# Gated linear attention and an expert layer on one core: TensorE's issue order written out as a pipeline over items, and eight PSUM banks for the later experts

## The chip, the cores and the metric

The kernel runs on one core of a Trainium2 chip. The metric is the device time of one execution in microseconds, the median over several executions. TensorE does the matrix products (its records are PE, its weight loads PEld), VectorE is DVE, ScalarE is ACT, GpSimd is POOL, and SyncE (SP) issues all DMAs of this kernel. Every engine works through its own instruction stream strictly in order, and waits on semaphores where an operand of another engine isn't there yet.

## What is computed

Two steps follow each other, here cut to what matters:

```python
# gated linear attention: q, k, v, f_logit are (4, 8, 768, 48), float32
f = sigmoid(f_logit); state = 0
for t in range(768):
    state = f[t][:, None] * state + outer(k[t], v[t])
    y[t] = q[t] @ state
x = y as (3072, 384)
# experts: w_gate (384, 8), w1 (8, 384, 1024), w2 (8, 1024, 384)
logits = x @ w_gate; P = exp(logits - logits.max())
for _ in range(8):
    P /= P.sum(1); P /= P.sum(0); P *= 3072 / 8
out = sum(P[:, e] * (relu(x @ w1[e]) @ w2[e]) for e in range(8))
```

The normalisation of P couples all tokens: no P is known before the last logits are, so an expert's output can be scaled only after all of the attention.

## The kernel before

**Attention.** The sequence work is cut into 32 items (batch, half of the sequence, pair of heads); four items, 4u to 4u+3, make the unit u of 384 tokens, and there are eight units. Every product of float32 operands is made of three float16 products (high times high, low times high, high times low), which is why most tiles come in pairs, as qh and ql. An item is prepared by `pre` and consumed by `attn`:

- `pre(i)`: ACT takes the sigmoids (L378, L380); DVE scans the decay (`r`, L382), guards and inverts it (`pi`, L384, L385), scales k (L394) and scans a second time (`q`, L386); POOL multiplies `tds` (L387) and q (L388); ACT rounds q to `qh` (L391) and DVE takes `ql` (L392); ACT and POOL make the two parts of k in `kb` (L398, L399), which a transposing DMA turns into `kt` (L401); ACT and DVE make `vh` and `vl` (L403, L404).
- `attn(i)`: 18 score matmuls into `aps` (L416), masked by DVE into `am` (L418) and split into `ah` (ACT, L421) and `al` (POOL, L422); 18 state matmuls into `kvps` (L429), folded by DVE into `ut` (L440), scaled by POOL (L444) and split into `sh` and `sl` (L445, L446); 33 or 36 output matmuls into `yps` (L457), which ACT and DVE evict as `xh` and `xl` (L463, L465).

After its fourth item a unit gets its gate logits (`logits`, L473 to L480): six matmuls over `xh` and `xl`, an ACT copy `lt`, three transposes, a DVE reduction into `lg`. When all eight units are done, `sinkhorn` normalises: eight rounds, each with one matmul (L92) between short DVE operations.

**Experts.** `moe(e, u)` takes expert e over the 384 tokens of unit u: 72 matmuls of 384 columns into eight `hps` tiles (L310), each evicted by ACT into `hh` (L315) and then by DVE into `hl` (L316); then 72 matmuls into three `yps` tiles (L329). I call this a pair, of 144 matmuls; there are 64 pairs. The pairs in RAW (experts 0 and 1, all units) are done before P is known: their result goes unscaled to DRAM (`yr`, `ys`) and is fetched again later (`yb`) and scaled and added. All other pairs add straight from PSUM (L294). The weights are loaded per expert in eight pieces (`load_w1`, `load_w2`) through two raw buffers and split: for experts 0 and 1 by ACT twice and POOL (L262 to L264), later by ACT and DVE (L266, L267), and DVE takes the largest magnitude of each piece (`wmx`, L268).

**What sets the order.** The program is written one step after another, and a scheduler orders each engine's stream by priority. Attention comes first in the text; `W1PRIO`, `W2PRIO` and `E0_HOLD` say how early the weights of experts 0 and 1 come. So the scheduler alone decides where expert matmuls stand between attention matmuls.

**PSUM.** Of eight banks the experts have three (pool `psm`, tag m); attention has five (pool `psa`: one for `aps`, two for `kvps`, two for `yps` and logits), and keeps them to the end of the program.

Of the kernel before, what the change touches and what calls it, by code (L numbers as in the profile page):

```python
# [74 lines left out]
def sinkhorn(nc, pool, psp, tag, identf, onesf, lg, pe):  # L75
# [2 lines left out]
    row = partition_reduce(nc, pool, psp, tag, identf, sm[:, 0:1], ALU.max, "sk")
# [1 line left out]
    nc.tensor.matmul(out=ps, lhsT=onesf[0:1, :], rhs=row, start=True, stop=True)  # L80
# [4 lines left out]
    for it in range(8):  # L85
# [6 lines left out]
        nc.tensor.matmul(out=ps, lhsT=onesf, rhs=cs, start=True, stop=True)  # L92
# [114 lines left out]
def fast(ctx, tc, qkf, vbd, wg, w1, w2, out, flag):  # L207
# [49 lines left out]
    def split_w(raw, e, j, k):  # L257
# [10 lines left out]
        nc.vector.tensor_reduce(out=wmx[:, k - 1, 4 * e + j:4 * e + j + 1], in_=wh.rearrange("p a f -> p (a f)"), axis=AX.X, op=ALU.max, apply_absolute_value=True)  # L268
# [26 lines left out]

    def moe(e, u, w, mode):
# [3 lines left out]
        for f in range(FT):  # L300
            if f % 2 == 0 and len(w1s) <= f // 2:
                with at(W1PRIO[e] if e < 2 else WPRIO + 10 * e):
# [3 lines left out]
            ps = psm.tile([128, HS], F32, name=f"hps_{e}_{u}_{f}", tag="m")  # L306
            n = 0
            for a, x in ((wh, xh), (wl, xh), (wh, xl)):
                for k in range(KT):
                    nc.tensor.matmul(out=ps, lhsT=a[:, k, fs], rhs=x[:, k, :], start=(n == 0), stop=(n == 8))  # L310
# [7 lines left out]
            hl.append(tl)  # L318
        for t in range(TT):
            ts = slice(t * 128, t * 128 + 128)  # L320
            ps = psm.tile([128, DM], F32, name=f"yps_{e}_{u}_{t}", tag="m")
            n = 0
            for f in range(FT):
                if f % 2 == 0 and len(w2s) <= f // 2:
                    with at(W2PRIO[e] if e < 2 else WPRIO + 10 * e):
                        w2s.append(load_w2(e, f // 2))
                wh, wl = w2s[f // 2]
                for a, b in ((hh[f], wh), (hl[f], wh), (hh[f], wl)):
                    nc.tensor.matmul(out=ps, lhsT=a[:, ts], rhs=b[:, f % 2, :], start=(n == 0), stop=(n == 3 * FT - 1))  # L329
# [36 lines left out]
    carry = [ap.tile([R, 96], F32, name=f"carry{p}", bufs=1) for p in range(NP)]  # L366
    tds = cst.tile([R, 32, NC], F32, name="tds")

    def pre(i):
# [12 lines left out]
        nc.vector.tensor_tensor_scan(out=r[:, ::-1], data0=ft[:, :0:-1], data1=ind[:, :0:-1], initial=0.0, op0=ALU.mult, op1=ALU.add)  # L382
# [9 lines left out]
        nc.vector.tensor_tensor(out=ql, in0=fl, in1=qh, op=ALU.subtract)  # L392
# [222 lines left out]
```

## Time and profile before

| | us |
|---|---|
| median of 3 runs (1740.84 to 1743.7) | 1742.46 |
| the profiled execution, its own time | 1744.41 |
| its span, first to last instruction | 1742.7 |
| last attention matmul (a logits transpose, L479) starts at | 385.2 |
| PE, DVE, ACT, POOL busy | 1625.3, 806.5, 476.7, 244.3 |

The span has two parts with different limits: up to about 385 us, where attention and expert matmuls share TensorE and DVE is the busiest engine, and the rest, where expert matmuls stand close together. A matmul's record lasts about 0.33 us, but the next one starts after half of that, since they are pipelined; so the distance from start to start is what counts, not the busy time.

### The profile page before, as it was taken

How to read it: one execution, taken by the hardware profiler on the slowest of the kernel's cores; microseconds unless marked ns; L12 is line 12 of the kernel's file. 1: busy time of each engine (PE TensorE's matmuls, PEld its weight loads, DVE VectorE, ACT ScalarE, POOL GpSimd, SP SyncE). 2: the span in 40 equal slices, each digit the busy share in tenths (PEclk: the TensorE clock that was granted, in tenths of full speed). 3: DMA queues.
4: the chain of work that ended last, by engine and by line, in shares of the span. 5: the costliest groups of instructions: out<-in, count | busy, mean ns of one | idle time of the engine just before them, and what ended most of it. 6: DMA issues, size and time to landing. Idle time of an engine off the chain costs nothing.

```text
span 1742.7 us, 27315 instructions
## 1 busy us (share of the span) xinstructions
PE 1625.3 (93%) x11566; PEld 1002.1 (58%) x11566; DVE 806.5 (46%) x1482; ACT 476.7 (27%) x956; POOL 244.3 (14%) x235
## 2 busy tenths in 40 slices
...
DVE  9999888855523642244222522253224422222222
...
PEclk9989999999999999999999999999999999999999
...
GB/s 178 136 172 142 120 129 109 110 54 29 127 50 73 156 84 1 1 28 46 1 1 1 73 1 1 1 55 19 1 1 28 28 1 1 1 5 24 28 28 29
DMA packets 90452, 90.26 MB, mean 52 GB/s; under 512 B 58960, under 2 KB 74448, under 8 KB 90320
## 3 DMA queue, kind: packets, MB, share of 16 engines
...
q14 instruction: 40, 0.33, 0.1%
...
## 4 chain that ended last, share of the span: by engine, by line
PE 76%; DVE 12%; DMA 5%; issue 2%; ACT 2%; POOL 2%; SPq 0%; ACTq 0%; DVEq 0%; POOLq 0%
PE yps L329 38%; PE hps L310 37%; DMA q<-in_qkf_dram 2%; DVE ql L392 1%; DVE q L386 1%; DMA w2r<-in_w_dram 1%; DVE r L382 1%; DVE vl L404 1%; DVE ut L440 1%; DVE wmx L268 1%; POOL kb L399 1%; DVE hl L316 1%; DVE xl L465 1%; DMA yb<-ys 1%; DVE w2l L267 1%
## 5 line engine op out<-in xcount | busy, mean ns | idle before, releaser
L315 ACT ACTIVATE hh<-hps 128x384 f16<-128x384 f32 x512 | 248.2, 488 | 939.1 <-PE hps L310 937.9
L329 PE MATMUL yps<-w2h,hh 128*128 128x384 f16 x1536 | 501.2, 328 | 0.6 <-DVE hl L316 0.6
L329 PE MATMUL yps<-w2h,hl 128*128 128x384 f16 x1536 | 494.2, 327 | 0.4 <-DVE hl L316 0.4
L329 PE MATMUL yps<-w2l,hh 128*128 128x384 f16 x1536 | 494.2, 328 | 0.0
L316 DVE SCALAR_TENSOR_TENSOR hl<-hps,hh 128x384 f16<-128x384 f32 x512 | 280.9, 555 | 401.4 <-ACT hh L315 400.7
L310 PEld LDWEIGHTS <-w1h 128*128 128x128 f16 x3072 | 301.1, 98 | 224.4 <-issue 32.9
L329 PEld LDWEIGHTS <-hh 128*128 128x128 f16 x3072 | 301.1, 98 | 198.0 <-issue 2.9
L310 PE MATMUL hps<-xh,w1h 128*128 128x384 f16 x1536 | 337.7, 329 | 21.5 <-DVE hl L316 21.2
L310 PE MATMUL hps<-xh,w1l 128*128 128x384 f16 x1536 | 336.9, 328 | 0.0
L310 PE MATMUL hps<-xl,w1h 128*128 128x384 f16 x1536 | 336.5, 328 | 0.0
L294 DVE SCALAR_TENSOR_TENSOR acc<-yps,pes,acc 128x384 f32<-128x384 f32 x144 | 88.9, 617 | 420.0 <-PE yps L329 420.0
L310 PEld LDWEIGHTS <-w1l 128*128 128x128 f16 x1536 | 151.0, 98 | 100.5 <-issue 2.7
L329 PEld LDWEIGHTS <-hl 128*128 128x128 f16 x1536 | 150.9, 98 | 100.5 <-issue 2.3
L399 POOL TENSOR_TENSOR kb<-q,kb 48x384 f16<-48x384 f32 x64 | 75.8, 1185 | 23.5 <-ACT kb L398 21.1
L429 PE MATMUL kvps<-vh,kt 128*128 128x96 f16 x384 | 39.0, 223 | 20.8 <-DVE ut L440 13.4
L429 PEld LDWEIGHTS <-kt 128*128 128x128 f16 x576 | 34.2, 107 | 33.3 <-issue 19.2
L334 ACT ACTIVATE yr<-yps 128x384 f32<-128x384 f32 x48 | 23.4, 486 | 91.5 <-PE yps L329 87.4
L416 PE MATMUL aps<-qh,kb 112*128 112x64 f16 x384 | 27.2, 204 | 21.9 <-ACT qh L391 16.9
L388 POOL TENSOR_TENSOR q<-q 112x384 f32<-112x384 f32 x32 | 44.7, 1396 | 18.9 <-DVE q L386 17.5
L416 PEld LDWEIGHTS <-kb 112*128 112x128 f16 x576 | 25.1, 105 | 38.3 <-issue 35.8
L457 PE MATMUL yps<-al,vh 128*128 128x64 f16 x192 | 35.0, 198 | 12.5 <-POOL al L422 11.9
L440 DVE SCALAR_TENSOR_TENSOR ut<-ut,tds,kvps 112x96 f32<-112x96 f32 x144 | 43.1, 301 | 2.3 <-PE kvps L429 1.3
...
## 6 DMA issues: line engine op xcount, KB each, us to landing
...
w1r<-in_w_dram SPq DMA_DIRECT2D x32, 384.0 KB, 3.3
w2r<-in_w_dram SPq DMA_DIRECT2D x32, 384.0 KB, 3.1
...
vs<-in_vbd_dram SPq DMA_DIRECT2D x4, 384.0 KB, 3.5
```

Source lines behind the costliest of these rows:

```text
L294: nc.vector.scalar_tensor_tensor(out=a, in0=y, scalar=p, in1=a, op0=ALU.mult, op1=ALU.add)
L310: nc.tensor.matmul(out=ps, lhsT=a[:, k, fs], rhs=x[:, k, :], start=(n == 0), stop=(n == 8))
L315: nc.scalar.activation(out=th, in_=ps, func=AF.Relu)
L316: nc.vector.scalar_tensor_tensor(out=tl, in0=ps, scalar=0.0, in1=th, op0=ALU.max, op1=ALU.subtract)
L329: nc.tensor.matmul(out=ps, lhsT=a[:, ts], rhs=b[:, f % 2, :], start=(n == 0), stop=(n == 3 * FT - 1))
L334: nc.scalar.activation(out=yr, in_=ps, func=AF.Copy)
L388: nc.gpsimd.tensor_tensor(out=fl, in0=fl, in1=q, op=ALU.mult)
L399: nc.gpsimd.tensor_tensor(out=kb[rs, 1, :, cs], in0=km[rs], in1=kb[rs, 0, :, cs], op=ALU.subtract)
L416: nc.tensor.matmul(out=aps[:, c, :], lhsT=a[:, c, :], rhs=x[:, cs[c]], start=(n == 0), stop=(n == 2))
L429: nc.tensor.matmul(out=kv[:, c, :], lhsT=ktb[i % 2][:, (a * NC + 3 * g + c) * R:(a * NC + 3 * g + c) * R + 128], rhs=x[:, 3 * g + c, :], s ...
L440: nc.vector.scalar_tensor_tensor(out=un, in0=ut[:, c, :], scalar=td[:, c:c + 1], in1=kv[0:R], op0=ALU.mult, op1=ALU.add)
L457: nc.tensor.matmul(out=yps[:, cs[c]], lhsT=a, rhs=x, start=(n == 0), stop=(n == len(mm) - 1))
```

## The change

1. Every matmul and transpose of the fast path goes through a helper `mm`, which ties it behind the one before it in the text. TensorE's stream is now the order of the text.
2. The text is a loop over items i = 0 to 32. A turn issues the score and state matmuls of item i (`scores`), from turn 5 on 28 expert matmuls, the output matmuls of item i-1 (`outputs`), after every fourth item the logits of the unit, and 28 more expert matmuls. `pre(i+1)` is written between. `moe` became a generator that yields after each matmul; `fill(n)` takes n of them from the RAW pairs.
3. In `sinkhorn`, 22 expert matmuls go ahead of each of its ten TensorE instructions.
4. RAW holds 13 pairs instead of 16 (expert 0 with all units, expert 1 with 0, 1, 2, 4 and 5). The other three pairs of expert 1 come after `sinkhorn` and add straight from PSUM.
5. DVE's first scan of `pre(i)` is tied behind a DVE operation of item i-1: `ql` for i = 1 to 3, `sl` of item 3 for i = 4, `am` of item i-1 from i = 5 on.
6. The 16 `wmx` reductions of experts 0 and 1 move from the place of the weights' loading to behind `pes`, the end of `sinkhorn`. All 16 weight pieces of experts 0 and 1 are issued in turns 0 to 8, with no `hold` and no priority of their own.
7. `psa` is closed when attention ends; five more banks (pool `psb`) go to the experts, which then use eight in turn (`bank`).

```diff
-RAW = [(e, u) for u in range(U) for e in range(2)]
+RAW = [(e, u) for u in range(U) for e in range(2) if e == 0 or u in (0, 1, 2, 4, 5)]
+FILL = 56
+SK_FILL = 22
...
+    def mm(transpose=False, **kw):
+        ins = (nc.tensor.transpose if transpose else nc.tensor.matmul)(**kw)
+        if order:
+            behind(ins, order[-1])
+        order.append(ins)
...
+    def largest(wh, e, j, k):
+        ins = nc.vector.tensor_reduce(out=wmx[:, k - 1, 4 * e + j:4 * e + j + 1], in_=wh.rearrange("p a f -> p (a f)"), axis=AX.X, op=ALU.max, apply_absolute_value=True)
+        if e < 2:
+            behind(ins, held[0])
...
+    def bank(shape, name):
+        n = banks[0]
+        banks[0] += 1
+        if late and n % 8 >= 3:
+            return late[1].tile(shape, F32, name=name, tag="m")
+        return psm.tile(shape, F32, name=name, tag="m")
...
+        if i:
+            behind(scan, done[i - 1])
...
+    for i in range(4 * U + 1):
+        if i < 4 * U:
+            scs[i] = scores(i, sts[i])
+        if i < 4:
+            ws[0][0].append(load_w1(0, i))
+        if i + 1 < 4 * U:
+            sts[i + 1] = pre(i + 1)
+        if 2 <= i < 6:
+            ws[0][1].append(load_w2(0, i - 2))
+        if 5 <= i < 9:
+            ws[1][0].append(load_w1(1, i - 5))
+            ws[1][1].append(load_w2(1, i - 5))
+        if i > 4:
+            fill(FILL // 2)
+        if i > 0:
+            outputs(i - 1, sts.pop(i - 1), scs.pop(i - 1))
+            if i % 4 == 0:
+                logits(i // 4 - 1)
+        if i > 4:
+            fill(FILL - FILL // 2)
+    sinkhorn(nc, cst, psa, "y", identf, onesf, lg, pe, lambda **kw: (fill(SK_FILL), mm(**kw)))
+    held.append(nc.vector.tensor_scalar(out=pes, in0=pe, scalar1=OSC, scalar2=None, op0=ALU.mult))
+    fill(10 ** 6)
     actx.close()
```

Three places in the engines' streams show what moves. Names end in a running number; `_1_0_5` in `hps_1_0_5` is expert 1, unit 0, row group 5. In the changed program every matmul stands under L224, the line of `mm`.

**TensorE, the logits of unit 1.** Before, from the last of the six logits matmuls (`lps1`, over `xl1`) to the transposes of its copy `lt1`:

```order
L473 MATMUL lps1_1120<-xl1_639,wgs_97 128x384
L310 LDWEIGHTS w1l_1_1_4482
L310 MATMUL hps_1_0_2_4487<-xh0_154,w1l_1_1_4482 128x384
L310 LDWEIGHTS w1l_1_1_4482
L310 MATMUL hps_1_0_2_4487<-xh0_154,w1l_1_1_4482 128x384
L310 LDWEIGHTS w1h_1_1_4481
L310 MATMUL hps_1_0_2_4487<-xl0_155,w1h_1_1_4481 128x384
L310 LDWEIGHTS w1h_1_1_4481
L310 MATMUL hps_1_0_2_4487<-xl0_155,w1h_1_1_4481 128x384
L310 LDWEIGHTS w1h_1_1_4481
L310 MATMUL hps_1_0_2_4487<-xl0_155,w1h_1_1_4481 128x384
L479 MATMUL lps21_1129<-identf_83,lt1_1127 128x16 x3
```

Five expert matmuls and their weight loads stood between the two, and others between the logits matmuls themselves. Now, from the last two logits matmuls on:

```order
L224 MATMUL lps1_1611<-xl1_938,wgs_94 128x384
L224 LDWEIGHTS wgs_94
L224 MATMUL lps1_1611<-xl1_938,wgs_94 128x384
L224 MATMUL lps21_1620<-identf_80,lt1_1618 128x16 x3
L224 LDWEIGHTS w1h_1_2_1306
L224 MATMUL hps_1_0_5_1560<-xl0_354,w1h_1_2_1306 128x384
L224 LDWEIGHTS w1h_1_2_1306
L224 MATMUL hps_1_0_5_1560<-xl0_354,w1h_1_2_1306 128x384
L224 LDWEIGHTS w1h_1_3_1513
```

The six logits matmuls follow the output matmuls of the unit's last item directly, and the transposes follow them with nothing between.

**DVE, around item 11.** Before, `ql12` and `ql13` (items 12 and 13) were done ahead of `am_11`, and the first scan of item 14 too:

```order
L392 TENSOR_TENSOR ql_12_1634<-q3_12_1620,qh_12_1633 112x384
L465 SCALAR_TENSOR_TENSOR xl2_1135<-yps_8_1216,xh2_1134 96x384
L418 SCALAR_TENSOR_TENSOR am_10_1412<-aps_10_1393,mask_90 128x384
L446 SCALAR_TENSOR_TENSOR sl0_140<-ut_10_1438,sh0_136 112x480
L404 SCALAR_TENSOR_TENSOR vl0_130<-vr_12_1622,vh0_124 128x576
L392 TENSOR_TENSOR ql_13_1753<-q3_13_1739,qh_13_1752 112x384
L465 SCALAR_TENSOR_TENSOR xl2_1135<-yps_9_1332,xh2_1134 96x384
L442 COPY ut_11_1554<-kvps_11_0_1534 112x96
L316 SCALAR_TENSOR_TENSOR hl_1_0_7_4584<-hps_1_0_7_4573,hh_1_0_7_4583 128x384
L440 SCALAR_TENSOR_TENSOR ut_11_1554<-ut_11_1554,tds_152,kvps_11_0_1534 112x96
L382 SCALAR_TENSOR_TENSOR r_14_1864<-ft0_113,ind_94 112x384
L418 SCALAR_TENSOR_TENSOR am_11_1528<-aps_11_1509,mask_90 128x384
```

Now, in the same place, between the second scan of item 11 and `am_11`:

```order
L474 SCALAR_TENSOR_TENSOR ut_10_1895<-ut_10_1895,tds_152,kvps_10_1_1885 112x96 x2
L474 SCALAR_TENSOR_TENSOR carry2_150<-ut_10_1895,tds_152,kvps_10_1_1885 112x96
L339 SCALAR_TENSOR_TENSOR hl_0_1_0_1952<-hps_0_1_0_1941,hh_0_1_0_1951 128x384
L339 SCALAR_TENSOR_TENSOR hl_0_1_1_1966<-hps_0_1_1_1955,hh_0_1_1_1965 128x384
L423 TENSOR_TENSOR ql_11_1919<-q3_11_1905,qh_11_1918 112x384
L480 SCALAR_TENSOR_TENSOR sl0_140<-ut_10_1895,sh0_136 112x480
L437 SCALAR_TENSOR_TENSOR vl0_130<-vr_12_2108,vh0_124 128x576
L510 SCALAR_TENSOR_TENSOR xl2_1781<-yps_9_1972,xh2_1780 96x384
L339 SCALAR_TENSOR_TENSOR hl_0_1_2_2016<-hps_0_1_2_1969,hh_0_1_2_2015 128x384
L339 SCALAR_TENSOR_TENSOR hl_0_1_3_2030<-hps_0_1_3_2019,hh_0_1_3_2029 128x384
L339 SCALAR_TENSOR_TENSOR hl_0_1_4_2044<-hps_0_1_4_2033,hh_0_1_4_2043 128x384
L450 SCALAR_TENSOR_TENSOR am_11_2070<-aps_11_2051,mask_87 128x384
```

`ql_11` is now the last preparation ahead of `am_11`; the first scan of item 12 comes behind it. Behind `ql_11` stand `sl0`, `vl0`, `xl2` and three evictions `hl` of expert rows.

**DVE, the end of `sinkhorn`.** Before, from `pes` on:

```order
L548 TENSOR_SCALAR pes_104<-pe_103 128x192
L507 TENSOR_REDUCE g_9359<-pe_103 128x1
L292 TENSOR_SCALAR acc0_7447<-yb_0_0_7448,pes_104 128x384 x3
L508 TENSOR_SCALAR ok_9357<-g_9359 128x1
L294 SCALAR_TENSOR_TENSOR acc0_7447<-yb_1_0_7453,pes_104,acc0_7447 128x384 x3
L292 TENSOR_SCALAR acc1_7704<-yb_0_1_7705,pes_104 128x384 x3
L294 SCALAR_TENSOR_TENSOR acc1_7704<-yb_1_1_7710,pes_104,acc1_7704 128x384 x3
L292 TENSOR_SCALAR acc2_7905<-yb_0_2_7906,pes_104 128x384 x3
L294 SCALAR_TENSOR_TENSOR acc2_7905<-yb_1_2_7911,pes_104,acc2_7905 128x384 x3
L292 TENSOR_SCALAR acc3_8106<-yb_0_3_8107,pes_104 128x384
L316 SCALAR_TENSOR_TENSOR hl_0_5_0_6282<-hps_0_5_0_6271,hh_0_5_0_6281 128x384
```

Now `pes` is followed by thirteen `wmx` reductions, of which these are the last ten, and then by the eviction of the last rows of the pair of expert 0 and unit 7:

```order
L285 TENSOR_REDUCE wmx_102<-w1h_0_3_578 128x1
L285 TENSOR_REDUCE wmx_102<-w1h_1_0_881 128x1
L285 TENSOR_REDUCE wmx_102<-w1h_1_1_1103 128x1
L285 TENSOR_REDUCE wmx_102<-w1h_1_2_1306 128x1
L285 TENSOR_REDUCE wmx_102<-w1h_1_3_1513 128x1
L285 TENSOR_REDUCE wmx_102<-w2h_0_0_480 128x1
L285 TENSOR_REDUCE wmx_102<-w2h_0_1_610 128x1
L285 TENSOR_REDUCE wmx_102<-w2h_0_2_733 128x1
L285 TENSOR_REDUCE wmx_102<-w2h_0_3_874 128x1
L285 TENSOR_REDUCE wmx_102<-w2h_1_0_888 128x1
L339 SCALAR_TENSOR_TENSOR hl_0_7_7_6748<-hps_0_7_7_6737,hh_0_7_7_6747 128x384
L285 TENSOR_REDUCE wmx_102<-w2h_1_1_1110 128x1
```

The scaled additions of the fetched results stood here before and now come later; the reductions, which had been spread over the loading of the weights, stand ahead of `hl_0_7_7`.

More of the change, by code (lines that the diff above doesn't have):

```diff
@@ L72, in partition_reduce, with sinkhorn @@
     return row
[L75 removed]
+def sinkhorn(nc, pool, psp, tag, identf, onesf, lg, pe, mm):
     sm = pool.tile([128, 2], F32, name="sk_sm")
     nc.vector.tensor_reduce(out=sm[:, 0:1], in_=lg.rearrange("p a e -> p (a e)"), axis=AX.X, op=ALU.max)
[L78 removed]
+    row = partition_reduce(nc, pool, psp, tag, identf, sm[:, 0:1], ALU.max, "sk", mm)
     ps = psp.tile([128, 1], F32, name="sk_m", tag=tag)
[L80 removed]
+    mm(out=ps, lhsT=onesf[0:1, :], rhs=row, start=True, stop=True)
     nc.vector.tensor_scalar(out=sm[:, 1:2], in0=ps, scalar1=-1.0, scalar2=None, op0=ALU.mult)
@@ L91, in sinkhorn @@
         ps = psp.tile([128, NE], F32, name=f"sk_c{it}", tag=tag)
-        nc.tensor.matmul(out=ps, lhsT=onesf, rhs=cs, start=True, stop=True)
+        mm(out=ps, lhsT=onesf, rhs=cs, start=True, stop=True)
         nc.vector.tensor_scalar(out=cs, in0=ps, scalar1=1e-9, scalar2=None, op0=ALU.add)
@@ L214, in at, with behind @@
         tc.cur_priority = kept
+    order, held = [], []
+    def behind(ins, first):
+        tc.add_manual_dep(
+            ins.ins, first.ins.name,
+            mybir.DependencyInfo(mybir.DependencyClass.NoSync, mybir.DependencyReason.DATA),
+            reason="issue order")
+    def mm(transpose=False, **kw):
[3 more added lines that the diff above has]
+        order.append(ins)
     cst = ctx.enter_context(tc.tile_pool(name="cst", bufs=1))
@@ L381, in pre @@
         r = ap.tile([R, HS], F32, name=f"r_{i}", tag="r")
-        nc.vector.tensor_tensor_scan(out=r[:, ::-1], data0=ft[:, :0:-1], data1=ind[:, :0:-1], initial=0.0, op0=ALU.mult, op1=ALU.add)
+        scan = nc.vector.tensor_tensor_scan(out=r[:, ::-1], data0=ft[:, :0:-1], data1=ind[:, :0:-1], initial=0.0, op0=ALU.mult, op1=ALU.add)
+        if i:
+            behind(scan, done[i - 1])
         r3 = r.rearrange("r (c t) -> r c t", t=C)
@@ L445, in attn, with outputs @@
         nc.scalar.activation(out=sh[:, c0:], in_=ut[:, c0:], func=AF.Copy, scale=SS)
-        nc.vector.scalar_tensor_tensor(out=sl[:, c0:], in0=ut[:, c0:], scalar=SS, in1=sh[:, c0:], op0=ALU.mult, op1=ALU.subtract)
+        ins = nc.vector.scalar_tensor_tensor(out=sl[:, c0:], in0=ut[:, c0:], scalar=SS, in1=sh[:, c0:], op0=ALU.mult, op1=ALU.subtract)
+        if i == 3:
+            done[i] = ins
+        return ah, al, shw, slw, c0
+    def outputs(i, st, sc):
+        u, p = i // 4, i % 4
+        qh, ql = st[2], st[3]
+        ah, al, shw, slw, c0 = sc
+        cs = [slice(c * C, (c + 1) * C) for c in range(NC)]
+        if p == 0:
+            xt[u] = xalloc(u)
         xh, xl = xt[u]
@@ L472, in logits @@
             for k in range(KT):
-                nc.tensor.matmul(out=ps, lhsT=wgs[:, k, :], rhs=x[:, k, :], start=(n == 0), stop=(n == 2 * KT - 1))
+                mm(out=ps, lhsT=wgs[:, k, :], rhs=x[:, k, :], start=(n == 0), stop=(n == 2 * KT - 1))
                 n += 1
```

97 lines of the change are left out of this document (52 added, 45 removed).

## The prediction

> **What bounds the kernel now.** I read the profile's head first, then busy time by stage, then expert matmuls alone before and after the last attention matmul.
>
> ```profile
> span 1742.7 us, 27315 instructions
> DVE  9999888855523642244222522253224422222222
> PEclk9989999999999999999999999999999999999999
> 50.00:100.00 50.00, 30.14 (x324) 21.80 (x323) 47.34 (x81) 27.62 (x53) 36.92 (x37) 0.93 0.55 140
> 385.30:1742.70 1357.40, 1337.74 (x8214) 803.78 (x8212) 472.89 (x848) 273.64 (x532) 0.00 (x0) 1.00 0.10 30
> 0.00:385.30 385.30, 98.74 (x522) 0.96 0.53 127
> 0.00:385.30 385.30, 93.31 (x504) 0.96 0.53 127
> 471.46 11.70 PE yps L329 x72
> 1724.82 11.71 PE yps L329 x72
> PE hps L310 <- DVE hl L316: 21.2, 22, 3.5
> ```
>
> The stage rows give length, then PE, PEld, DVE, ACT and POOL. Early on DVE is busy 47 of 50 us: it bounds the attention. The two rows up to 385.3 are the matmuls of L310 and of L329: 522 + 504 = 1026 of 9216 expert matmuls were issued by then. The chain of waits shows 72 of them in 11.70 us, so 0.1625 us each. The other 8190 need 1330.9 of the remaining 1357.4 us. Of the 26.5 left, the tail from the last matmul's end (1724.82 + 11.71 = 1736.5) to the end of the span takes 6.2. Most of the other 20 are the 21.2 us in which `hps` waited for `hl`: three banks were full. So 20 us can be had behind the attention; ahead of it, TensorE's idle time and the order.
>
> **What the new order fixes.** Turns 5 to 32 of the loop issue 28 x 56 = 1568 expert matmuls. The other 7648 take 7648 x 0.1625 = 1242.8 us. The time is therefore T, the end of the loop, + 1242.8 + the stalls behind the loop + 6.2. Before, matmul 1568 would have been issued at 385.3 + 542 x 0.1625 = 473.4 plus its stalls; that is what T competes with.
>
> **A turn on TensorE.** One dense run of output matmuls gives 0.030 us each:
>
> ```profile
> 363.59 2.09 PE yps L457 x70
> ```
>
> 18 score and about 35 output matmuls of 64 columns take 53 x 0.030 = 1.6; 18 state matmuls of 96 columns, by columns, 0.045 each (estimate), 0.8; 56 expert matmuls 9.1. Together 11.5 us: no turn can be shorter.
>
> **A turn on DVE, ACT and POOL.** Since the scan of item i+1 now stands behind `am` of item i, the whole preparation lies inside the turn. Rows give minimum/median/maximum in ns, or, from the groups, busy us and mean ns:
>
> ```profile
> L382 DVE TENSOR_TENSOR_SCAN r<-ft,ind x32: 923/958/3189, 6.7 to 335.8; 112x384 f32<-112x384 f32 x32
> L386 DVE TENSOR_TENSOR_SCAN q<-ft,pi x32: 939/1096/2629, 9.5 to 339.8; 112x384 f32<-112x384 f32 x32
> L394 DVE SCALAR_TENSOR_TENSOR q<-q,r x32: 543/546/1264, 7.8 to 337.6; 112x384 f32<-112x384 f32 x32
> L399 POOL TENSOR_TENSOR kb<-q,kb x64: 899/1114/3552, 9.3 to 359.8; 48x384 f16<-48x384 f32 x64
> L388 POOL TENSOR_TENSOR q<-q x32: 986/1208/4023, 12.0 to 340.8; 112x384 f32<-112x384 f32 x32
> L392 DVE TENSOR_TENSOR ql<-q,qh x32: 525/1049/3099, 17.6 to 346.8; 112x384 f16<-112x384 f32 x32
> L404 DVE SCALAR_TENSOR_TENSOR vl<-vr,vh x32: 722/750/3651, 8.9 to 357.1; 128x576 f16<-128x576 f32 x32
> L446 DVE SCALAR_TENSOR_TENSOR sl<-ut,sh x32: 640/750/1692, 42.1 to 371.0; 112x480 f16<-112x480 f32 x16, 112x576 f16<-112x576 f32 x16
> L398 ACT ACTIVATE kb<-q 48x384 f16<-48x384 f32 x64 | 33.1, 517 | 11.1 <-issue 3.4 <-DVE q L394 3.2 <-PE aps L416 3.2
> L391 ACT ACTIVATE qh<-q 112x384 f16<-112x384 f32 x32 | 16.4, 511 | 9.5 <-POOL q L388 9.4
> L440 DVE SCALAR_TENSOR_TENSOR ut<-ut,tds,kvps 112x96 f32<-112x96 f32 x144 | 43.1, 301 | 2.3 <-PE kvps L429 1.3
> L384 DVE TENSOR_SCALAR pi<-r 112x6 f32<-112x6 f32 x32 | 13.1, 410 | 0.3
> L465 DVE SCALAR_TENSOR_TENSOR xl<-yps,xh 32x384 f16<-32x384 f32 x24 | 13.3, 553 | 6.7 <-ACT xh L463 6.0
> L316 DVE SCALAR_TENSOR_TENSOR hl<-hps,hh 128x384 f16<-128x384 f32 x512 | 280.9, 555 | 401.4 <-ACT hh L315 400.7
> ```
>
> From the end of `am`: `r` 0.96, a `ut` 0.30, `pi` 0.41, the scaling of k 0.55: 2.2. Then ACT's first `kb` 0.52 and POOL's two `kb` 2.2 reach 4.9; q on POOL stands behind them, 1.2, to 6.1; `qh` 0.5, to 6.6. The second scan holds POOL back by some 0.6 (median against minimum of these rows), so 7.2; `ql` 1.05, to 8.25. Then `vl` and `sl` 0.75 each, `xl` 0.55, to 10.3, and the next `am`, 0.55 (the `xl` row), to 10.85. Up to two `hl` before `ql` fill DVE's waiting time and cost nothing; one behind it costs 0.555. By the order of the changed program, of the 20 turns from `am` 5 to `am` 31 without logits, 7 have none behind `ql`, 3 have one, 3 two, 5 three, 2 four. With max(11.5, 10.85 + 0.555 n) this is 80.5 + 34.5 + 36 + 62.6 + 26.1 = 240. In the 7 turns with three or four, TensorE itself finds no free bank among three until the first of them; I add 0.6 each: 244, or 12.2 a turn. Bounds: 11.5 a turn, and 13.5 if POOL stretches DVE as below.
>
> **A turn with logits.** In six turns (8, 12, ... 28) logits follow `outputs`, and TensorE cannot go past them.
>
> ```profile
> L476 ACT ACTIVATE lt<-lps 16x384 f32<-16x384 f32 x8 | 3.8, 477 | 11.4 <-PE lps L473 9.8 <-PE kvps L429 1.6
> L473 PE MATMUL lps<-xl,wgs 128*128 128x384 f16 x24 | 7.3, 325 | 1.9 <-DVE xl L465 1.8
> 458.50:462.30 3.80, 0.28 (x2) 1.00 0.80 235
> 463.50:466.90 3.40, 3.40 (x13) 0.50 0.58 181
> ```
>
> DVE reaches the third `xl` at 8.25 + 1.5 + 1.65 = 11.4. The last logits matmul 0.33, `lt` 0.48, three transposes and hand-overs 0.5: 12.7. Only then come 28 expert matmuls, 4.55, the next scores with their latency 0.75, and `am` 0.55: 18.6. In the trace of before, logits waited 1.8 us for `xl` in all, since other matmuls stood between. The last two rows (PE time, then the granted clock) show another price: after 3.8 us with next to no matmul, TensorE ran at clock 0.50 for 3.4 us, which costs up to 1.7. Here it idles some 7 us with a few matmuls in between; I take a third of it, 0.6: 19.2 a turn, bounds 17 and 20.5. [...]
>
> **The first five items and the last turns.**
>
> ```profile
> L418 DVE SCALAR_TENSOR_TENSOR am<-aps,mask x32: 516/547/558, 20.5 to 366.3; 128x384 f32<-128x384 f32 x32
> L264 POOL TENSOR_TENSOR w1l<-w1r,w1h 128x768 f16<-128x768 f32 x8 | 13.5, 1689 | 0.1
> w1r<-in_w_dram SPq DMA_DIRECT2D x32, 384.0 KB, 3.3
> ```
>
> `am` 0 starts at 20.5; the 31 after it took 345.8 us, 11.2 each. The five turns up to `am` 5 have no expert matmuls, but POOL has about twelve weight pieces to subtract in them, 1.69 each, and each raw buffer is free again only after 3.3 of DMA, two ACT passes and that subtraction; ACT and POOL wait for these in order, with `qh` and q behind them. I take 11.0 a turn: 21 + 55 = 76. Bounds: 68 if the loads hide, 86 if they hold up every turn. After `am` 31 come three fills of 4.55, two sets of outputs of 1.05, the eviction of the last unit and its logits (about 4), and the last fill: 24.5. T = 76 + 244 + 6 x 19.2 + 24.5 = 459.7.
>
> **Behind the loop.**
>
> ```profile
> L268 DVE TENSOR_REDUCE wmx<-w1h 128x1 f32<-128x768 f16 x32 | 30.2, 945 | 1.6 <-ACT w1h L263 1.6
> L92 PEld LDWEIGHTS sk_c<-sk_cs,onesf 128*128 128x128 f32 x16 | 2.8, 190 | 0.5
> L92 PE MATMUL sk_c<-sk_cs,onesf 128*128 128x8 f32 x16 | 2.3, 214 | 0.0
> L82 ACT ACT_TABLE_LOAD x1 | 1.3, 1283 | 0.0
> L267 DVE SCALAR_TENSOR_TENSOR w1l<-w1r,w1h 128x768 f16<-128x768 f32 x24 | 23.0, 957 | 3.4 <-ACT w1h L266 3.4
> ```
>
> `sinkhorn`: 22 expert matmuls, 3.6 us, cover each round's DVE chain but not the small matmul and its weight load, 0.40, ten times; the exponential with its table load comes once, 2: 6 us (0 to 10). Then DVE has thirteen `wmx` of 0.945, 12.3 us, ahead of `hl_0_7_7`. With what precedes them (the round's last steps, an `hl`, `pes`) that `hl` ends 14.8 us after the last `sk_c`. TensorE needs it after 34 matmuls, 5.5: it stands for 9.3. This cover was there before, since the 16 reductions were spread over the attention; it is gone. Then expert 2's eight splits (0.957 and 0.945 each) stand among the evictions of the next pair, for which I count 6 more, and a window at half clock, 1.7: 17 (10 to 25). In return the 20 us of waits for `hl` of before go: with eight banks, 72 `hps` matmuls run before the first must be freed. So the eight banks are worth 20 us, and the 6 + 17 of new stalls take as much.
>
> **The sum.** 459.7 + 1242.8 + 6 + 17 + 6.2 = 1731.7, against a span of 1742.7 before. That span is the median of the runs (1742.46) to 0.3; the profiled execution's own 1744.41 lies 1.7 above its span. I give 1732, 0.6% less.
>
> **Rivals.**
>
> 1. *POOL sets the turn (slower).* Two rows of before, DVE's, then POOL's, lie over each other:
>
> ```profile
> 21.81 3.65 DVE L404 SCALAR_TENSOR_TENSOR vl<-vr,vh 128x576 f16<-128x576 f32 x1
> 21.61 3.24 POOL L264 TENSOR_TENSOR w1l<-w1r,w1h 128x768 f16<-128x768 f32 x2
> ```
>
> DVE's 0.75 us `vl` became 3.65 while POOL ran two subtractions. `r`, the second scan, `ql`, `vl` and `sl` have such maxima too. Before, preparations ran items ahead, so a stretch cost throughput only; now it sits on the chain inside the turn. At 13.5 a plain turn and 20.5 with logits, 26 + 8 us are added: 1766. It decides from 12.7 a plain turn, where the sum is 1742. Against it: the medians (0.96 for `r`) are near the minima. [...]
>
> 2. *TensorE sets the turn (faster).* If `hl` fit into DVE's waits, plain turns take 11.5, logits turns 17 and the first five reach 70: 14 + 13 + 6 us less, 1699. For it: DVE's work in a turn, some 10 us, is under 11.5. Against it: 32 `hl` stand behind `ql`.
>
> 3. *Nothing is left (same).* The stalls behind the loop come to 27 and more instead of 17, because `yb` and expert 2's DMAs wait with them: 1742.
>
> That the order or the banks are not what the change says is no rival: the streams show both.
>
> **Chances and range.** My forecast 0.45, rival 1 0.22, rival 2 0.22, rival 3 0.11. A difference under 0.2%, 3.5 us, is about what a measurement of this kernel can tell from none. Of my forecast's 0.45 (its own range 1714 to 1750), 0.36 lies below 1739, 0.06 within and 0.03 above. Rival 2 adds 0.22 and rival 3 0.01 to faster; rivals 1 and 3 add 0.02 and 0.05 to the same, 0.20 and 0.05 to slower. Faster 0.59, same 0.13, slower 0.28. The range 1703 to 1762 leaves out the outer ends of rivals 1 and 2, about 0.2.
>
> **What would show it.** The distance from `am` to `am`: 12 us without logits, 19 with (11.5 and 17: rival 2; 13.5: rival 1). TensorE's wait in logits turns named `xl` and `lt`, some 7 us each. A wait of `yps` for `hl` of about 9 us behind `sinkhorn`, with `wmx` running. No waits of `hps` for `hl` at later changes of expert. If the loop ends before 440 or after 475 us, or the 9 us wait isn't there, the prediction's working is wrong even if its time is right.

## The result and the profile after

The changed kernel takes 1766.95 us (median of 4 runs, 1763.77 to 1769.03), the kernel before 1743.08 on the same chip: a ratio of 1.0136 with a 95% interval from 1.0116 to 1.0156. It is slower by 1.4%, where 0.6% faster was forecast. The page of the changed kernel has, against the rows shown of before:

```profile
span 1767.2 us, 27188 instructions
DVE  8766566656659652225222532244222522222222
PEclk9898889889999999999999999999999999999999
```

DVE is no longer full in the first stage, so it does not bound the attention any more. The clock row has changed too: in the first ten slices it dips to 8 six times, before once.

**Which term failed.** The sum had two halves: the end of the loop, and what lies behind it. The 1568 expert matmuls of the loop have all been issued at 494.5 us, and the last of the 9216 starts at 1761.0, 6.2 us before the end. Busy time by stage, in the columns that the prediction explained (the last three are clock, DMA share and GB/s):

```profile
83.00:494.50 411.50, 361.61 (x3553) 229.26 (x3551) 257.87 (x533) 176.65 (x378) 158.99 (x174) 0.92 0.35 88
494.50:1761.00 1266.50, 1249.78 (x7672) 749.72 (x7669) 468.37 (x830) 248.44 (x481) 0.00 (x0) 1.00 0.09 28
```

Behind the loop, 1266.5 less 1242.8 of matmuls is 23.7 us of stalls; the prediction had 6 + 17 = 23. So the sum of that half was right to a microsecond. The loop was to end at 459.7 and ended at 494.5: these 34.8 us are the whole error, and they lie beyond the 475 us from which the prediction itself called its working wrong. The starts of `am` on DVE divide them up (`am` 5, 8, 9, 10 and 31; start, then duration):

```profile
83.03 0.55 DVE L450 SCALAR_TENSOR_TENSOR am<-aps,mask 128x384 f32<-128x384 f32 x1
...
125.88 0.55 DVE L450 SCALAR_TENSOR_TENSOR am<-aps,mask 128x384 f32<-128x384 f32 x1
147.27 0.56 DVE L450 SCALAR_TENSOR_TENSOR am<-aps,mask 128x384 f32<-128x384 f32 x1 [0.75 <-PE aps L224]
158.65 0.56 DVE L450 SCALAR_TENSOR_TENSOR am<-aps,mask 128x384 f32<-128x384 f32 x1 [1.48 <-PE aps L224]
...
465.87 0.56 DVE L450 SCALAR_TENSOR_TENSOR am<-aps,mask 128x384 f32<-128x384 f32 x1 [0.58 <-PE aps L224]
```

The first five items end at 83.0 (76 forecast). The logits turn from 125.88 to 147.27 takes 21.4, the plain turn behind it 11.4. Over all 26 such turns: 20 plain ones take 251.2 (12.56 each; 244 forecast), six with logits 131.6 (21.9 each; 115.2 forecast). From the last `am` to the end of the loop it is 28.6 (24.5). So 7.0 + 7.2 + 16.4 + 4.1 = 34.7, with the logits turns the largest.

**The first suspect: the clock.** TensorE in one logits turn, and the busy time around it: ahead of the fall of the clock, behind it, and once more behind it in three steps:

```profile
129.78 0.33 PE L224 MATMUL hps<-xl,w1h 128*128 128x384 f16 x1
...
134.94 1.49 PE L224 MATMUL lps<-xh,wgs 128*128 128x384 f16 x3 [3.76 <-ACT xh L508]
136.54 1.65 PE L224 MATMUL lps<-xl,wgs 128*128 128x384 f16 x3
138.82 0.50 PE L224 MATMUL lps<-identf,lt 16*128 16x16 f32 x3 [0.63 <-ACT lt L521]
...
139.86 1.17 PE L224 MATMUL hps<-xh,w1h 128*128 128x384 f16 x3
140.82 1.17 PE L224 MATMUL hps<-xh,w1l 128*128 128x384 f16 x3
```

```profile
131.00:134.60 3.60, 0.18 (x7) 0.09 (x3) 2.65 (x7) 2.27 (x6) 2.10 (x3) 1.00 0.52 98
134.60:144.80 10.20, 8.85 (x27) 3.60 (x27) 4.92 (x8) 2.92 (x7) 0.00 (x0) 0.50 0.28 79
134.60:138.00 3.40, 2.68 (x6) 0.52 (x5) 2.55 (x5) 1.25 (x3) 0.00 (x0) 0.50 0.83 233
138.00:141.40 3.40, 2.77 (x11) 1.43 (x11) 1.80 (x3) 1.18 (x3) 0.00 (x0) 0.50 0.01 3
141.40:144.80 3.40, 3.40 (x12) 1.65 (x11) 0.56 (x1) 0.49 (x1) 0.00 (x0) 0.50 0.00 0
```

TensorE waits 3.76 us for `xh`. The clock then falls to 0.50 at 134.6 and stays there for 10.2 us, three times the 3.4 us that the prediction had read from the trace of before. (That trace has seven more such windows ahead of 300 us, one of them of 6.8 us, from 88.1 on; the prediction passed them over.) In the window from 134.6 on, three `hps` matmuls take 0.96 (139.86 to 140.82) instead of 0.49. All eight units' logits are followed by such a window, six of 10.2 us and the last two of 6.8. The windows are two or three steps of 3.41 us long, and whole steps lie between their starts: 17 from 134.6 to 192.6, and 18 from there to 254.1. In the turn shown TensorE works for 2.68 and 2.77 us of the first two steps and the clock doesn't come back; it comes back after the step that is full. The prediction had taken 0.6 us a turn for this.

Up to the transposes the forecast of this turn held, though the wait is named `xh`, of ACT, and not `xl`: they end at 139.32, 13.4 us after the start of `am`, where 12.7 from its end was forecast. (In the other five such turns it is 13.4 to 14.6 us, and once 17.3.) From there to the next `am` the forecast was 4.55 + 0.75 = 5.3 us; it took 7.95 here, and 6.6 to 8.0 in the six turns.

**The second suspect: a wait on ACT that the prediction had no term for.** From the sums of waits after (engine, line, what for, total us, times, longest):

```profile
ACT tds L409 <- DMA q<-in_qkf_dram: 74.2, 25, 5.0
PE lps L224 <- ACT xh L508: 24.2, 17, 3.8
PEld lps L224 <- ACT lt L521: 17.7, 8, 4.2
PE lps L224 <- ACT lt L521: 10.2, 8, 3.3
PE hps L224 <- DVE hl L339: 8.3, 9, 2.1
```

ACT stands 74 us in 25 turns in front of `tds`, which needs the load of an item whose first scan comes two or three turns later. What stands behind `tds` in ACT's stream waits too:

```profile
214.52 0.85 ACT L338 ACTIVATE hh<-hps 128x384 f16<-128x384 f32 x2
218.30 0.21 ACT L409 ACTIVATE tds<-q 112x6 f32<-112x6 f32 x1 [2.93 <-DMA q<-in_qkf_dram]
218.42 0.85 ACT L338 ACTIVATE hh<-hps 128x384 f16<-128x384 f32 x2
```

Two evictions `hh` come only behind it, at 218.42. In ACT's stream an `hh` comes directly behind such a wait nine times, an `ah` and an `lt` five times each. In the kernel before a row of the same kind was there, for `ft`, with half the time (what it cost there was not tried):

```profile
ACT ft L378 <- DMA q<-in_qkf_dram: 36.5, 21, 3.6
```

### The profile page after: what moved, and what is told of

The parts are those of the page before. It is cut to its first block, busy times and chain, and to the rows that moved or that the text cites. A ratio compares the mean times of both kernels' runs of the same rounds, so it can differ in the third digit from the quotient of the medians.

```text
span 1767.2 us, 27188 instructions
## 1 busy us (share of the span) xinstructions
PE 1638.3 (93%) x11566; PEld 1001.1 (57%) x11566; DVE 793.7 (45%) x1482; ACT 475.0 (27%) x947; POOL 219.7 (12%) x231
## 4 chain that ended last, share of the span: by engine, by line
PE 71%; issue 5%; DVE 4%; POOL 4%; DMA 3%; ACT 1%; SPq 0%; POOLq 0%; DVEq 0%; ACTq 0%
PE yps L224 35%; PE hps L224 35%; POOL kb L432 2%; DMA yb<-ys 1%; DMA q<-in_qkf_dram 1%; POOL q L419 1%; DVE wmx L285 1%; POOL al L456 1%; POOL ut L478 1%; DVE acc L306 1%; DVE hl L339 0%; DVE r L411 0%; DVE q L427 0%; DMA kt<-kb 0%; ACT hh L338 0%
## 5 line engine op out<-in xcount | busy, mean ns | idle before, releaser
L224 PE MATMUL yps<-w2h,hl 128*128 128x384 f16 x1536 | 505.9, 329 | 15.1 <-DVE hl L339 15.0
L224 PE MATMUL yps<-w2h,hh 128*128 128x384 f16 x1536 | 505.8, 329 | 3.1 <-DVE hl L339 3.1
L224 PE MATMUL yps<-w2l,hh 128*128 128x384 f16 x1536 | 505.6, 329 | 0.0
L224 PEld LDWEIGHTS <-w1h 128*128 128x128 f16 x3072 | 301.3, 98 | 208.8 <-issue 15.9
L224 PEld LDWEIGHTS <-hh 128*128 128x128 f16 x3072 | 302.3, 99 | 200.9 <-issue 8.1
L224 PE MATMUL hps<-xh,w1h 128*128 128x384 f16 x1536 | 338.1, 329 | 9.1 <-DVE hl L339 8.3
L224 PE MATMUL hps<-xl,w1h 128*128 128x384 f16 x1536 | 337.9, 329 | 0.0
L224 PE MATMUL hps<-xh,w1l 128*128 128x384 f16 x1536 | 337.9, 329 | 0.0
L306 DVE SCALAR_TENSOR_TENSOR acc<-yps,pes,acc 128x384 f32<-128x384 f32 x153 | 94.5, 617 | 433.5 <-PE yps L224 433.5
L224 PEld LDWEIGHTS <-hl 128*128 128x128 f16 x1536 | 151.4, 99 | 121.8 <-DVE hl L339 18.1
L224 PEld LDWEIGHTS <-w1l 128*128 128x128 f16 x1536 | 150.9, 98 | 100.5 <-issue 3.4
L432 POOL TENSOR_TENSOR kb<-q,kb 48x384 f16<-48x384 f32 x64 | 72.4, 1131 | 11.9 <-ACT kb L431 9.4
L224 PE MATMUL aps<-qh,kb 112*128 112x64 f16 x384 | 24.5, 201 | 36.1 <-ACT qh L422 35.1
L423 DVE TENSOR_TENSOR ql<-q,qh 112x384 f16<-112x384 f32 x32 | 30.1, 940 | 45.7 <-ACT qh L422 45.7
L224 PEld LDWEIGHTS <-kb 112*128 112x128 f16 x576 | 23.8, 103 | 44.5 <-issue 16.2
L431 ACT ACTIVATE kb<-q 48x384 f16<-48x384 f32 x64 | 33.2, 519 | 32.9 <-DVE q L427 30.4
L478 POOL TENSOR_TENSOR ut<-ut,tds 112x480 f32<-112x480 f32 (+1 forms) x32 | 39.8, 1244 | 5.2 <-DVE carry L474 4.1
L224 PE MATMUL kvps<-vh,kt 128*128 128x96 f16 x384 | 32.4, 220 | 8.5 <-DMA kt<-kb 8.5
L417 DVE TENSOR_TENSOR_SCAN q<-ft,pi 112x384 f32<-112x384 f32 x32 | 37.9, 1185 | 0.1
```

What stands on the lines that cost most here:

```text
L224: ins = (nc.tensor.transpose if transpose else nc.tensor.matmul)(**kw)
L306: nc.vector.scalar_tensor_tensor(out=a, in0=y, scalar=p, in1=a, op0=ALU.mult, op1=ALU.add)
L417: nc.vector.tensor_tensor_scan(out=fl, data0=ft[:, 0:HS], data1=pi.rearrange("r c t -> r (c t)"), initial=0.0, op0=ALU.mult, op1=ALU.add)
L423: ins = nc.vector.tensor_tensor(out=ql, in0=fl, in1=qh, op=ALU.subtract)
L431: nc.scalar.activation(out=kb[rs, 0, :, cs], in_=km[rs], func=AF.Copy)
L432: nc.gpsimd.tensor_tensor(out=kb[rs, 1, :, cs], in0=km[rs], in1=kb[rs, 0, :, cs], op=ALU.subtract)
```

## The experiments

Theory A: the logits' waits, and the half clock that follows them, made the loop longer. Theory D was formed after e4, since e1 had shown that moving the logits removes only half of it: ACT's wait at `tds` has a share of its own. Rivals: DVE, ACT and POOL set the turn whatever TensorE does (B), and the clock falls by itself (C). In the table stand the median, its ratio to the kernel before on the same chip with its 95% interval, the time at which 1568 expert matmuls had been issued (the loop's end, except in the last row), and from there to the last expert matmul.

| kernel | us | ratio to before | 1568 issued | rest |
|---|---|---|---|---|
| before | 1743.08 | 1 | 480.4 | 1255.8 |
| the change | 1766.95 | 1.0136 (1.0116 to 1.0156) | 494.5 | 1266.5 |
| e1 logits late | 1744.41 | 1.0024 (1.0009 to 1.0038) | 470.3 | 1265.2 |
| e2 busy wait | 1754.29 | 1.0081 (1.0053 to 1.0110) | 479.6 | 1266.7 |
| e3 three banks | 1778.67 | 1.0219 (1.0191 to 1.0248) | 491.3 | 1278.7 |
| e4 `wmx` spread | 1756.72 | 1.0098 (1.0066 to 1.0130) | 490.2 | 1254.6 |
| e5 `tds` behind `ft` | 1748.51 | 1.0031 (1.0021 to 1.0040) | 472.1 | 1266.4 |
| e6 before, eight banks | 1732.73 | 0.9940 (0.9924 to 0.9957) | 477.5 | 1243.9 |
| e7 = e1 + e4 + e5 | 1715.17 | 0.9835 (0.9818 to 0.9851) | 453.5 | 1254.4 |
| e8 = e2 + e5 | 1734.69 | 0.9964 (0.9950 to 0.9977) | 460.9 | 1265.1 |
| e9 = e7, `xmx` later | 1705.49 | 0.9786 (0.9760 to 0.9811) | 444.5 | 1254.4 |
| e10 = e9, 62 fills | 1700.35 | 0.9761 (0.9739 to 0.9782) | 431.6 | 1261.4 |

The chips' medians of before differ by up to 3 us, so gains are taken from the ratios (0.001 is 1.7 us). The loop is the same in the change, e3 and e4, and ended at 494.5, 491.3 and 490.2: some 4 us of its end is chance.

**e1, logits behind the second fill.**

```diff
             outputs(i - 1, sts.pop(i - 1), scs.pop(i - 1))
-            if i % 4 == 0:
-                logits(i // 4 - 1)
         if i > 4:
             fill(FILL - FILL // 2)
+        if i > 0 and i % 4 == 0:
+            logits(i // 4 - 1)
```

> Logits stand behind the turn's second 28 expert matmuls instead of ahead of them. Theory A (the logits' waits for xl and lt, 41 us of gaps on TensorE in seven turns, and the half-clock windows that follow each of them, 25 us, are what made the loop longer than forecast): the waits shrink to 10 to 15 us in all (the hand-over over lt stays), no window at clock 0.50 longer than 3.4 us is left between 90 and 480 us, a logits turn takes 13 us, time 1715 to 1728. Rival B (the chain over DVE, ACT and POOL sets the turn; logits only show it): the wait comes back in front of the next scores or hidden matmuls, time 1752 or more. Rival C (the clock drops by itself after some 50 us of dense matmuls): the waits go but the windows at clock 0.50 stay at the same distance, about 1740.

The gain is 0.0112, 19.5 us, half of what A expected at the least, and a logits turn takes 18.1 us, where 13 was expected. The logits' waits went as forecast, but another grew:

```profile
ACT tds L409 <- DMA q<-in_qkf_dram: 68.8, 24, 5.4
...
PE hps L224 <- DVE hl L339: 17.4, 11, 4.3
PEld lps L224 <- ACT lt L521: 14.0, 8, 3.9
...
PE lps L224 <- ACT xh L508: 2.6, 3, 2.3
```

`xh` fell from 24.2 to 2.6, while the hidden matmuls' wait for a free bank rose from 8.3 to 17.4. So A holds in part, and B in part: something on ACT or DVE comes late even where logits don't ask for it. Against C: of the seven long windows at clock 0.50 between 90 and 494 us only five are left up to 470, at other distances, 3.4 to 10.2 us long (A had expected none above 3.4).

**e2, the same wait, but with TensorE busy.** Its 28 extra matmuls give nothing that is used; the real ones overwrite them.

```diff
+        for _ in range(28):
+            mm(out=ps, lhsT=wgs[:, 0, :], rhs=ws[0][0][0][0].rearrange("p a f -> p (a f)")[:, 0:HS], start=True, stop=True)
         n = 0
         for x in (xh, xl):
```

> Adds 28 matmuls of 384 columns (4.55 us) that only fill TensorE's wait ahead of each unit's logits; their result is overwritten. Theory A: the wait is filled, the windows at clock 0.50 go, and what follows runs at full clock: 12 to 20 us faster than the change, 1747 to 1755; what is left of the logits' price is the wait. Rival C: the windows stay, time 1767 or more. If the wait alone were the price and the half clock were free: 1767, within 3.

Adding 224 matmuls made it faster, by 0.0055, 9.6 us; the loop ended 14.9 us earlier. The stage row shows the clock:

```profile
83.00:479.60 396.60, 372.16 (x3736) 243.88 (x3734) 260.07 (x534) 177.14 (x378) 159.18 (x174) 0.98 0.38 92
```

The mean clock in the loop rises from 0.92 to 0.98, and the wait for `xh` falls from 24.2 us to 0.5. So in this loop it is TensorE's waiting that brings the clock down, and rival C is out. The gain, 9.6 us by the ratio and 14.9 by the loop's end, is what the half clock costs, less whatever the filling matmuls themselves delay.

**e3, three banks.**

```diff
-        if late and n % 8 >= 3:
+        if False:
```

> The later experts rotate through three PSUM banks as before; all else as in the change. If the eight banks are worth the 12 us of gaps of hidden matmuls that the kernel before has behind 480 us, and also cover part of the waits behind sinkhorn: 1779 to 1787. Rival (the wait only moves from a bank to hl, which the output matmuls need anyway): 1770 or less.

Slower than the change by 0.0083, 14 us, and the stage behind the loop is 12.2 us longer. So the banks are worth 12 to 14 us.

**e4, the largest-weight reductions one by one.**

```diff
+            if pend and (e == 1 and f % 2 and pend[0][1] == 0 or e == 2 and f % 4 == 3):
+                behind(largest(*pend.pop(0)), ev)
```

(`ev` is the `hl` just issued; the 16 reductions wait in `pend` instead of being issued together.)

> The sixteen reductions of the largest weights of experts 0 and 1 no longer stand together ahead of hl_0_7_7: those of expert 0 come one behind every second hl of pairs (1,3) and (1,6), those of expert 1 two per unit of expert 2. Theory (DVE's queue makes the 8.3 us stall and its half-clock window): that stall goes, the later ones of 8 us behind (1,3) get no longer, 9 to 13 us less, 1754 to 1758. Rival (DVE is full through these pairs, with the raw sums and expert 2's splits, so the stall only moves): 1763 to 1767.

The stage behind the loop is 11.9 us shorter, as the theory said (e7 and e9, which have this edit too, give the same 1254.4 there). The ratio alone would not show it: it falls by 0.0038, 7 us, with an interval from about 0 to 13. What the edit removes stood in the change as the prediction had it; DVE first, then TensorE:

```profile
536.48 6.96 DVE L285 TENSOR_REDUCE wmx<-w1h 128x1 f32<-128x768 f16 x8
543.36 4.38 DVE L285 TENSOR_REDUCE wmx<-w2h 128x1 f32<-128x768 f16 x5
547.66 0.55 DVE L339 SCALAR_TENSOR_TENSOR hl<-hps,hh 128x384 f16<-128x384 f32 x1
```

```profile
548.27 0.50 PE L224 MATMUL yps<-w2h,hl 128*128 128x384 f16 x1 [7.95 <-DVE hl L339]
```

Thirteen `wmx`, then `hl`, and TensorE waits 7.95 us for it.

**e5, `tds` behind `ft` on ACT.** One edge in ACT's order, no work added or removed (`sig` is the large sigmoid, `ft`).

```diff
-        nc.scalar.activation(out=td, in_=fl3[:, :, 0], func=AF.Sigmoid)
+        behind(nc.scalar.activation(out=td, in_=fl3[:, :, 0], func=AF.Sigmoid), sig)
```

> On ACT the small sigmoid of an item's first columns (tds) is ordered behind its large one (ft); all else as in the change. In the change tds waits 74 us in 25 turns for the load of an item that is needed two turns later, and the evictions hh are queued behind it. Theory D (those waits delay hh, and through it hl and the free banks): tds no longer waits, TensorE's gaps between hidden matmuls in the loop, 11 us, fall below 4, the logits' waits stay; 7 to 15 us faster than the change, 1752 to 1760. Rival (ACT's waits lie beside waits that are there anyway): within 3 us of 1767.

A gain of 0.0105, 18 us, more than expected; the loop ended 22.4 us earlier. In its sums of waits the `tds` row is gone, and these are the rows of the others:

```profile
PE lps L224 <- ACT xh L508: 22.4, 24, 2.7
...
PEld lps L224 <- ACT lt L521: 13.3, 8, 2.5
PE lps L224 <- ACT lt L521: 5.8, 8, 1.6
...
PE hps L224 <- DVE hl L339: 4.6, 4, 1.9
ACT ft L407 <- DMA q<-in_qkf_dram: 2.9, 2, 1.6
```

ACT now waits 2.9 us for that load in all. The rows for `lt` and `hl` fall by 4 each, and turns get shorter throughout (plain ones 11.92, with logits 20.6). Theory D holds. Some of the gain comes through the clock, since shorter waits leave 48 us at clock 0.50 between 90 and 494 us instead of 65; e8 tells the two apart.

**e6, the other part of the change alone:** the kernel before with the same rule for banks, `psa` closed behind the raw pairs.

```diff
+        if len(late) > 1 and n % 8 >= 3:
+            return late[1].tile(shape, F32, name=name, tag="m")
```

> The kernel before with the second part of the change alone: eight PSUM banks once the raw pairs are written out. If the banks are worth what the gaps of hidden matmuls behind 480 us say (12 us, most of it at the changes of expert), 9 to 13 us faster than before. Rival (without the kernel's own order the waits only move to hl or to expert 2's splits): 0 to 4 us.

Faster than before by 0.6%, 10 us. So of the change's two parts the banks gain 10 to 14, and all the rest of it (the order, fewer raw pairs, the moved reductions) loses 2.2%, 38 us (e3 against before).

**e7, three edits at once:** those of e1, e4 and e5.

> Logits behind the second fill, the largest-weight reductions spread, and tds behind ft, all three. If their gains add (22, 12 and 11 us): 1722, and under 1728 in any case; the gaps of 22 us between hidden matmuls that came when the logits moved shrink to 10 or less by theory D. If those gaps are DVE's work in the turn rather than ACT's wait: they stay near 20, 1730 or more.

The gain is 0.0301 against 0.0255 for the three apart, which agrees within their intervals: they add. The loop ends at 453.5. The hidden matmuls still wait 13.3 us for `hl`, between what the two theories expected. One logits turn of it shows what still holds TensorE, DVE first:

```profile
289.52 0.93 DVE L424 TENSOR_TENSOR ql<-q,qh 112x384 f16<-112x384 f32 x1 [2.81 <-ACT qh L423]
290.38 0.75 DVE L438 SCALAR_TENSOR_TENSOR vl<-vr,vh 128x576 f16<-128x576 f32 x1
291.81 0.76 DVE L481 SCALAR_TENSOR_TENSOR sl<-ut,sh 112x576 f16<-112x576 f32 x1 [0.69 <-ACT sh L480]
292.60 1.69 DVE L511 SCALAR_TENSOR_TENSOR xl<-yps,xh 32x384 f16<-32x384 f32 x3
294.30 1.35 DVE L556 TENSOR_REDUCE xmx<-xh 128x3 f32<-128x1152 f16 x1
295.69 1.49 DVE L338 SCALAR_TENSOR_TENSOR hl<-hps,hh 128x384 f16<-128x384 f32 x3
```

```profile
296.30 0.98 PE L224 MATMUL hps<-xh,w1h 128*128 128x384 f16 x3 [4.57 <-DVE hl L338]
```

Three banks are full, and three `hl` stand behind everything that DVE does in that turn. One of these, `xmx`, is needed only by the bound on the inputs, long after.

**e8, both suspects removed, all else as in the change:** `tds` behind `ft`, and the 28 filling matmuls (whose results are overwritten).

> The change with tds behind ft and with the 28 filling matmuls ahead of each unit's logits (their result is overwritten). If the two misses of the prediction are ACT's wait (18.5 us alone) and the half clock behind the logits' wait (12.7 us alone), and they add: 1734 to 1738, within 6 us of the time that was forecast without them. If they are one and the same thing seen twice: 1745 or more.

1734.69 us. The loop ends at 460.9, where 459.7 was forecast; its stage runs at full clock:

```profile
83.00:460.90 377.90, 363.92 (x3734) 240.69 (x3733) 266.05 (x533) 178.24 (x378) 161.24 (x174) 1.00 0.41 96
```

The two are separate and add: 0.0172 against 0.0055 + 0.0105. On top of e2, where the clock is 0.98 already, the edge of e5 still gives 0.0117, 20 us; on top of e5 the filling gives 0.0067, 11 us. And from the last transpose to the next `am` it is now 5.2 us in five of the six logits turns, where 5.3 was forecast and the change took 6.6 to 8.0.

**e9, the eight `xmx` behind pair (3,0)**, and **e10, 62 fills a turn** with pair (1,3) among the raw ones.

```diff
-            nc.vector.tensor_reduce(out=xmx[:, u, :], in_=xt[u][0], axis=AX.X, op=ALU.max, apply_absolute_value=True)
+            behind(nc.vector.tensor_reduce(out=xmx[:, u, :], in_=xt[u][0], axis=AX.X, op=ALU.max, apply_absolute_value=True), last[0])
```

(`last[0]` is the latest `hl` when pair (3,0) is done.) For e10:

```diff
-RAW = [(e, u) for u in range(U) for e in range(2) if e == 0 or u in (0, 1, 2, 4, 5)]
-FILL = 56
+RAW = [(e, u) for u in range(U) for e in range(2) if e == 0 or u in (0, 1, 2, 3, 4, 5)]
+FILL = 62
```

> As the kernel with late logits, spread reductions and tds behind ft (1715.2), and the eight reductions xmx, 1.35 us each on DVE, go from the logits turns to behind pair (3,0). In that kernel they stand between xl and the evictions hl for which TensorE waits 3 to 5 us in a logits turn. If DVE's queue is what holds these: 6 to 9 us less, 1706 to 1710. If the wait is on ACT or on the transposes: within 2 us of 1715.

> As e9, with 62 expert matmuls in a turn instead of 56 and pair (1,3) among the raw ones, so that they last to the end of sinkhorn. If a plain turn is longer than its matmuls (12.1 us against 11.5), the six more, 0.98 us, cost about 0.4 a turn and take 0.98 from behind: 8 to 15 us less than e9. If the turn is set by TensorE, or the added evictions lengthen it as much: within 3 us of e9.

e9 gains another 0.0049, 8.5 us, as the theory said: DVE's queue held the `hl`. e10 gains 0.0025, 4 us, less than forecast and with intervals that touch; its plain turns take 13.0 us against 12.0, all of the added 0.98, so there was little idle time left to fill in them. e10 is the fastest kernel here: 2.4% faster than before, 3.7% faster than the change (0.9761 to 1.0136).

## Why the prediction was wrong

**The step that failed: "A turn with logits", and there the clock.** This term was mis-sized. The prediction took "a third of it, 0.6" for the half clock, 3.6 us in the six turns. Filling the wait makes these six turns shorter by 10.6 us (e2) and by 9.9 (e8 against e5), and all of the loop by 11 to 15. The reason given was that a few matmuls stand in the wait. They did not keep the clock up: it fell to 0.50 at 134.6 behind 3.6 us with 7 matmuls (0.18 us of work), and at 192.6 behind 3.8 us with 10 (0.88). The duration was wrong as well: 10.2 us, not 3.4, in most turns. The window that the prediction read ended after one full step; in the change short waits went on into the first two steps.

A window at 0.50 follows the logits' wait of all eight units, although TensorE had up to 1.9 us of work in the 3.4 us ahead of it (1.94 ahead of 486.2). With the whole 1.7 that the prediction had read from the trace of before, instead of a third of it, its sum would have been 7 us more, nearer to what was measured but still 28 us short.

**The step that was missing: ACT's own order.** "A turn on DVE, ACT and POOL" had only the instructions that the next scores need. It left out one, `tds`, that waits for a load and has others queued behind it, and so put this wait at nothing. It costs 18 us (e5). The kernel before had a row that pointed at it, `ft` for `q`, 36.5 us, and the prediction passed it over. In the fixed order `lt` is awaited by the very next matmuls, and `hh`, through `hl`, by the hidden matmuls that need its bank.

**What offset.** With both removed (e8) the loop ends within 1.2 us of the forecast; so the two make up 33.6 of the 34.8 us. That it comes so close is in part luck, since it is not so term by term: first items 83.1 instead of 76, plain turns 236.5 instead of 244, logits turns 113.8 instead of 115.2, the end 27.5 instead of 24.5. The plain turns had been put too long by as much as the first items had been put too short. The first items lay in their bounds (68 to 86); why they take 7 us more was not tried.

**What was right.** The wait behind `sinkhorn` (9.3 forecast, 7.95 measured, with the thirteen `wmx` ahead of `hl`), the sum of the stalls behind the loop (23 and 23.7), no waits at later changes of expert (the row below holds the changes to experts 2 to 7, the first at 638 us, and TensorE is busy throughout), and the tail. The terms of the 23 hold too: beyond 0.1625 us a matmul, `sinkhorn` costs 4.4 us (6 forecast), the stretch with the thirteen `wmx` 9.5 (9.3), that with expert 2's splits 8.0 (6), and the last window at half clock 1.7 (1.7). The eight banks were put at 20 us and are worth 10 to 14. The prediction gave them the 21.2 us in which `hps` waited for `hl`, but only 12.8 of these lie behind 385.3 us, and 9.3 behind 480.4. In the table, the kernel before has 1255.8 - 1242.8 = 13.0 us of stalls in its rest, and e6 has 1.1.

```profile
609.10:1761.00 1151.90, 1151.90 (x7092) 692.75 (x7089) 381.84 (x640) 221.95 (x432) 0.00 (x0) 1.00 0.06 19
```

**The rivals.** Rival 1 gave 1766, the measured time, by luck: its reason, that POOL stretches DVE and so sets the turn, did not come about. Three of the rows that should have stretched, after (minimum, median, maximum in ns):

```profile
L411 DVE TENSOR_TENSOR_SCAN r<-ft,ind x32: 945/948/2395, 6.0 to 454.3; 112x384 f32<-112x384 f32 x32
L417 DVE TENSOR_TENSOR_SCAN q<-ft,pi x32: 941/1096/1667, 9.2 to 457.6; 112x384 f32<-112x384 f32 x32
L423 DVE TENSOR_TENSOR ql<-q,qh x32: 546/820/2834, 15.6 to 461.6; 112x384 f16<-112x384 f32 x32
```

Their medians are not above those of before (958, 1096, 1049), and plain turns took 12.56 on average, under its point of 12.7. An edge on ACT alone, with POOL's work unchanged, then brought them to 11.92 (e5). What the rival rested on does show in single instructions, as in `ql` beside POOL's `ut`; DVE, then POOL:

```profile
238.97 0.93 DVE L423 TENSOR_TENSOR ql<-q,qh 112x384 f16<-112x384 f32 x1 [1.66 <-ACT qh L422]
238.34 1.15 POOL L478 TENSOR_TENSOR ut<-ut,tds 112x576 f32<-112x576 f32 x1
```

`ut` ends at 239.49 and `ql` 0.41 us later, and so it is in the turn at 165.72, where `ut` takes 0.99 and `ql` 0.77. In both, `ql` takes 0.2 to 0.4 us more than its minimum of 0.55. That is too little to set the turn. Rival 2 did not come true either: without the two suspects plain turns take 11.8 (e8), close to TensorE's 11.5, so for these turns it was near, but those suspects decided first. Rival 3 asked for 27 us of stalls behind the loop; there are 23.7.
